# A convolution, router and mixture of experts on one core: later preparation of one visit, another pace of the routing behind the convolution, additions that no longer wait their turn

## The chip, the core and the metric

The kernel runs on one core of a Trainium2 chip. The metric is the device time of one execution in microseconds (us). Engines are named as in the profile: PE (matrix multiply), PEld (its weight loads), DVE (vector), ACT (scalar), POOL (general), SP (issues most DMAs). Each engine takes its instructions strictly in the order in which they were written; a wait holds all that stands behind it on the same engine.

## The reference

`x` is 8 x 2880 x 192. A softmax over 7 taps gives each token and head its own weights, and a causal convolution sums 7 shifted rows with them. Each of the 23040 rows then goes to one of 16 experts (first the best of 4 groups, then the best of 4 experts in it), through two matrices with a ReLU between them, and is scaled by its gate.

```
out = np.einsum('bshk,bskhg->bshg', w, x_unf)          # w: softmax of weight_gen over k (7 taps)
g_idx = np.argmax(x @ w_group, axis=1)                 # group, then expert in the group
e_idx = np.argmax(xg @ w_expert[g], axis=1)
h = np.maximum(xg[mask_e] @ w1[g, e], 0.0)             # 192 -> 1024
ye = h @ w2[g, e]                                      # 1024 -> 192
out[tok_idx] = combined[:, None] * ye                  # gate of the group times gate of the expert
```

## The kernel before

**Front.** Sixteen groups of tokens (12 or 6 columns of 128) go through the convolution on DVE (`conv`: products at L318, additions at L338), the softmax (`softmax`), and the router (`route`), which counts the rows of each expert and gives every row its place. `scatters` writes the rows to a buffer in HBM sorted by expert: for every two columns DVE makes the places (`pair`, L591) and POOL issues two indirect DMAs (L622). Behind the last group `ending` writes 16 pads (L610) after the rows of the 16 experts. `front()` is a generator: each step emits a little DVE work. Three queues hang on it: `side` (softmax), `routes` (router and tables) and `spread` (scatters and pads).

**Visits.** The experts' work is a list of 103 visits in 14 rounds; a round may begin once the rows of certain groups lie in HBM. Visits 0 to 9 take one unit of 128 rows ("plain"), visits 10 to 95 two units (256 rows) of which 86 to 95 are in the last round, and 96 to 102 one unit again. Visits of the last round read rows that all scatters and pads must have reached. A visit is four units of PE work (`u` 0 to 3): in each, `gemm1` (L1021, five terms of high and low parts in a two-unit visit) and, two units later, `gemm2` (L1048, or L1050 and L1051 where the second matrix is split too, visits 52, 57, 61, 64, 68, 70, 72 and 74 to 95). ACT does the ReLU, `finish` scales the sum on ACT (L1057) and, in a split visit, adds the second half on DVE (L1063); then `send` lets POOL scatter the result (L1065). The next `gemm2` needs the accumulator that these free.

**Preparation.** In units 0 and 1 of a visit the next is prepared: `prep_d` copies a part of its rows `xb` to `xd` (ACT L981), `prep_x` transposes them on PE (L997, L998, tile `tpx`), ACT and DVE make `xh` and `xlo`. Weights of a two-unit visit land in `raw` (SP, L910 and L913) and are split on ACT (`hi`, L935 and L938) and DVE (`lo`, L953). The rows `xb` are loaded at L892. SP issues all of these; a load of rows waits on SP until the scatters it depends on have landed.

**Who sets the order.** PE, ACT, DVE and SP run in the order in which Python emits the instructions, and a planner decides that order with a clock of its own, `clk`. `fill(until)` steps `front()` until the planned DVE time reaches `until`; a yielded `NEXT` ends it for this unit. `after`, `delay` and `delay_more` put work on lists that `flush` empties, and each item first calls `fill(t + HOP)`, so front work is emitted ahead of it up to its planned time `t`. `move(queue, q, most)` takes up to `most` steps from a queue entry and stops at one that waits for the next unit. A load is asked for (`ask`) and emitted by `pump` once the planner believes that its rows have come; at unit 0 of a visit `pump(units[...][0])` insists on the next one, and `need` then steps `front()` until its table and rows are emitted:

```
def need(n):
    while not ready(n):
        state["starve"] = True
        more = step() is not False
```

Weights of a visit are asked for by expert number, which the same readiness guards (`if not ready(a[0]) ...: continue`). The last loop of `front()` runs once the convolution is finished; the same happens behind every group through `finish_all`.

Of the kernel before, what the change touches and what calls it, by code (L numbers as in the profile page):

```python
# [34 lines left out]
def conv_moe_kernel(ctx: ExitStack, tc: tile.TileContext, x, wgen, w_group, w_expert, w1, w2, out):  # L35
# [21 lines left out]
    NU = NFT // 2  # L57
# [18 lines left out]
    left = (NTOK - sure + NE * (BK - 1)) // BK  # L76
# [162 lines left out]
    NEXT = object()  # L239
# [60 lines left out]
    def softmax0():  # L300
        wt = grp[0].wt
        m, z = (cv.tile([P, SG * H, 1], F32, name=name, bufs=1) for name in "mz")
        a, b = slice(0, SC * H), slice(SC * H, SG * H)
        for c in (a, b):
            yield from powers(wt[:, c], m[:, c])
        yield from norms(wt[:, a], z[:, a])
        soft0.append([norms(wt[:, b], z[:, b]), None])

    sums, evac, spread = [], [], []
# [433 lines left out]
    def lower_part():  # L743
        t = next(lows[0][0], None)
        if t is None:
            lows.clear()
        else:
            lows[0][1] = t
# [16 lines left out]
    def front():  # L765
        side, routes = [], []
        load_group(0)
        set_up()
        load_group(1)
        yield from softmax0()  # L770
        lows.append([remainders(), 0.0])
        lower_part()
        for g in range(ENDS[-1]):
            o = grp[g]
            routes.append([route(g, o), None])
            state["urgent"] = g == FIRST
            loads = [] if g in (0, ENDS[-1] - 1) else [(0, 0), (8, 1)] if g < MAIN else [(6, 0), (13, 1)]
            ahead = 4 if g <= FIRST else 12 if g < MAIN else 17

            def soft():  # L780
                if not o.ahead and g + 1 < ENDS[-1]:
                    o.ahead = True
                    side.append([softmax(g + 1), None])

            for n, c in enumerate(conv(g, o)):
                yield c
                if loads and n >= loads[0][0]:
                    load_group(g + 1, loads.pop(0)[1])
                if n >= ahead:
                    soft()  # L790
                for q in list(soft0):
                    yield from move(soft0, q, 1)
                if not state["urgent"]:
                    for q in side[:1]:
                        yield from move(side, q, 3)
                for q in spread[:1]:
                    yield from move(spread, q, 1)
                if routes:
                    yield from move(routes, routes[0], HURRY if FIRST <= g < MAIN else 3 if g < FIRST else 8 if g in ENDS else 2)
            while loads:  # L800
                load_group(g + 1, loads.pop(0)[1])
            soft()
            yield from finish_all(side)
            yield from finish_all(routes, 1)
            yield from finish_all(spread, 1)
        while routes:
            for q in spread[:1]:
                yield from move(spread, q, 1)
            q = routes[0]
            yield from move(routes, q, 4)  # L810
            if routes and q[1] is not None:
                yield Until(q[1][1]) if q[1][0] == "time" else NEXT

    def finish_all(qs, keep=0):
        while len(qs) > keep:
# [5 lines left out]
    def move(qs, q, most):  # L821
        for _ in range(most):
            if q[1] is not None:
                what, v = q[1]
                if what == "time" and v > clk["dve"] or what == "unit" and v == state["unit"] and most != HURRY or what == "chunk" and v.o.chunks < v.n:
                    return
                q[1] = None
            c = next(q[0], None)
            if c is None:
                qs.remove(q)  # L830
                return
            if c is NEXT:
                q[1] = "unit", state["unit"]
            elif isinstance(c, Chunk):
                q[1] = "chunk", c
            elif isinstance(c, Until):
                q[1] = "time", c
            else:
                yield c

    fr = front()

    def step():
# [25 lines left out]
    def ready(n):  # L869
        return order[n][:2] in arrive  # L870

    def plain(n):
        return order[n][1] == 1
# [85 lines left out]
    def after(t, cost, note, f, *a, **k):  # L959
        late.append(doing(t, cost, note, f, a, k))  # L960
# [7 lines left out]
    def flush():  # L968
        for q in (late, held):
            while q:  # L970
                q.pop(0)()
        held.extend(later)
        later[:] = far
        far.clear()
# [78 lines left out]
    def finish(b):  # L1053
        for t in range(b.nt):
            gate = b.x[:, t, D:D + 1]
            y = b.x[:, t, 0:D]
            nc.scalar.activation(out=y, in_=b.py[t][:, 0:D], func=AF.Copy, scale=gate)  # L1057
            ty = run("act", 0.3, b.ty)
            after(ty, 0.0 if b.o.whole else 0.35, None, send, b, t, y)

    def send(b, t, y):
        if not b.o.whole:
# [19 lines left out]
    def blocks_of(n):  # L1082
        return max(1, order[n][1] // 2)
# [6 lines left out]
    def blocks(n0, n1, paced):  # L1090
        want, jobs = [], []

        def pump(upto=None):
            for a in list(want):
                if a[1] == 0 and upto is None and ready(a[0]):
                    r = order[a[0]][0]
                    if arrive[order[a[0]][:2]] - (8.0 if r == 1 else 0.0) > max(clk["pe"], clk["dve"]):
                        continue
                if upto is not None and a[0] <= upto:
                    need(a[0])  # L1100
                if not ready(a[0]) or a not in want:
                    continue
                want.remove(a)
                load(*a)
# [34 lines left out]
        units = []  # L1139
# [4 lines left out]
        def block(i):  # L1144
            n, j, _ = units[i]
            o = visits[n]
            b = Slot()
            b.th = {}
            b.plain = plain(n)
            b.nt = 1 if b.plain else 2  # L1150
            b.n = b.nt * P
            b.o, b.h, b.x = o, {}, o.xb[:, 2 * j:2 * j + b.nt, :]
            if not b.plain:
                while state["open"]:
                    assert step() is not False
                state["slots"] = True
            return b
# [29 lines left out]
        for i in range(len(units) + LAG):  # L1187
            if i < len(units):
                n, j, u = units[i]
                gemm1(cur, u)  # L1190
                queue.append((cur, u))
                if i + NU - u < len(units):
                    if u == 0:
                        pump(units[i + NU][0])
                        nxt = block(i + NU)
                        prep_d(nxt)
                    if u == 1:
                        prep_x(nxt, (i + NU) // NU)
                if u == NU - 1 and i + 1 < len(units):
                    cur = nxt  # L1200
            asks = []
            if i >= LAG:
                b, u = queue.pop(0)
                gemm2(b, u)
                if u == NU - 1:
                    finish(b)
                    if i - LAG + 1 < len(units) and units[i - LAG + 1][0] != units[i - LAG][0]:
                        asks.append(units[i - LAG][0] + 3)
            if i < len(units):
                n, j, u = units[i]  # L1210
                nb = blocks_of(n)
                at = j * NU + u
                end = at == nb * NU - 1
                if end and n + 3 < n1 and plain(n + 3):
                    ask_w(n + 3)
                if end and n + 4 < n1 and plain(n + 2) and not plain(n + 4):
                    ask_w(n + 4)
                did = 0
                for job in list(jobs):
                    m, part, h = job  # L1220
                    if m > n + 2 or (part == 3 and (m > n + 1 or at < LAG)):
                        continue
                    must = end and m == n + 1
                    if not must and (did >= 1 or (m, part + (h if part == 3 else 0)) in want or not ready(m)):
                        continue
                    jobs.remove(job)
                    work_split(job)
                    did += 1
                state["unit"] += 1
            flush()  # L1230
            if paced:
                fill(clk["pe"] + AHEAD[0 if cur.plain else 1 if cur.o.whole else 2])
            for a in asks:
                ask_x(a)
            pump()
# [40 lines left out]
```

## Time and profile before

| | |
|---|---|
| median of 3 runs | 1193.42 us (1193.22 to 1197.89) |
| profiled execution, own time | 1198.05 us |
| its span, first to last instruction | 1196.2 us |
| granted clock of PE, mean over the span | 0.986 |
| PE busy, share of the span | 96% |
| DVE, ACT, POOL busy | 80%, 56%, 38% |

The own time is 1.85 us longer than the span. The profiled execution is 4.6 us above the median and close to the slowest of the three timed runs. Times of rows count from the start of the span. A busy PE is not a PE at full clock: where the granted clock is 0.50, the same matmuls take twice as long.

### The profile page before, as it was taken

How to read it: one execution, taken by the hardware profiler on the slowest of the kernel's cores; microseconds unless marked ns; L12 is line 12 of the kernel's file. 1: busy time of each engine (PE TensorE's matmuls, PEld its weight loads, DVE VectorE, ACT ScalarE, POOL GpSimd, SP SyncE). 2: the span in 40 equal slices, each digit the busy share in tenths (PEclk: the TensorE clock that was granted, in tenths of full speed). 3: DMA queues.
4: the chain of work that ended last, by engine and by line, in shares of the span. 5: the costliest groups of instructions: out<-in, count | busy, mean ns of one | idle time of the engine just before them, and what ended most of it. 6: DMA issues, size and time to landing. Idle time of an engine off the chain costs nothing.

```text
span 1196.2 us, 26069 instructions
## 1 busy us (share of the span) xinstructions
PE 1144.0 (96%) x9047; PEld 1113.8 (93%) x9047; DVE 953.2 (80%) x1728; ACT 671.9 (56%) x1267; POOL 455.9 (38%) x411
## 2 busy tenths in 40 slices
PE   4998997999999999999999999999999899999995
PEld 4777997999999999999999999999999899999995
DVE  7987786899999989989899898889876766777600
ACT  2533334655655655656565665655667576777631
POOL 3061350263636253344545253454534443221111
PEclk9999998999999999999999999999999999999998
DMA  9677599989897898888779694899676699887891
GB/s 248 222 234 222 160 311 259 293 245 291 243 284 220 264 272 274 225 276 242 261 215 317 191 301 138 253 281 254 186 212 181 194 283 288 243 221 215 222 257 33
DMA packets 181263, 284.99 MB, mean 238 GB/s; under 512 B 16519, under 2 KB 141293, under 8 KB 180992
## 3 DMA queue, kind: packets, MB, share of 16 engines
q1 hardware_dynamic: 160536, 239.53, 69.9%
q0 software_dynamic: 19184, 39.22, 10.1%
q10 hardware_dynamic: 1400, 4.47, 1.3%
q8 instruction: 73, 1.20, 0.4%
q14 instruction: 70, 0.57, 0.2%
HBM read 239.81 MB, written 44.23 MB: 237 GB/s over the span
## 4 chain that ended last, share of the span: by engine, by line
PE 81%; issue 6%; DMA 5%; DVE 3%; ACT 2%; POOL 1%; ACTq 0%; POOLq 0%; SPq 0%
PE ph L1021 34%; PE py L1048 26%; PE py L1050 6%; PE py L1051 3%; PE pl L409 2%; PE tpx L998 1%; PE tpx L997 1%; DMA raw<-in_moe_w 1%; DMA rows<-xrow,posi 1%; PE tp L437 1%; PE ph L731 1%; DVE pr L318 1%; DMA xb<-rows 1%; PE ph L359 1%; DMA xin<-in_x 1%
## 5 line engine op out<-in xcount | busy, mean ns | idle before, releaser
L1021 PE MATMUL ph<-xh,wa 128*128 128x256 f32 x2064 | 456.0, 298 | 0.0
L1065 POOL DMA_INDIRECT out<-xb x189 | 229.2, 1213 | 521.1 <-ACT xb L1057 321.7
L1048 PE MATMUL py<-wc,hh 128*128 128x192 f32 x2096 | 391.1, 327 | 9.4 <-ACT xb L1057 7.0
L1021 PE MATMUL ph<-xlo,wa 128*128 128x256 f32 x1376 | 356.4, 282 | 1.0 <-DVE xlo L953 1.0
L1021 PEld LDWEIGHTS ph<-xh,wa 128*128 128x128 f32 x2064 | 348.3, 190 | 4.9 <-issue 3.4
L1048 PEld LDWEIGHTS py<-wc,hh 128*128 128x128 f32 x2096 | 336.1, 191 | 9.8 <-ACT xb L1057 7.2
L1027 ACT ACTIVATE hh<-ph 128x512 f32<-128x512 f32 (+1 forms) x296 | 162.3, 548 | 272.0 <-PE ph L1021 270.4
L1021 PEld LDWEIGHTS ph<-xlo,wa 128*128 128x128 f32 x1376 | 259.8, 189 | 1.3 <-DVE xlo L953 1.2
L318 DVE TENSOR_TENSOR pr<-xin,wt 128x1152 f32<-128x1152 f32 x187 | 250.5, 1351 | 8.7 <-PE tpx L359 5.1
L622 POOL DMA_INDIRECT rows<-xrow,pair x138 | 161.7, 1171 | 102.7 <-DVE pair L591 49.3
L338 DVE TENSOR_TENSOR xrow<-xrow,pr 128x1152 f32<-128x1152 f32 x138 | 186.6, 1352 | 0.4
L1050 PE MATMUL py<-wc,hh 128*128 128x384 f32 x464 | 142.8, 363 | 3.4 <-DVE xb L1063 3.4
L953 DVE SCALAR_TENSOR_TENSOR hl<-ph,hh 128x512 fp32r<-128x512 f32 x116 | 80.0, 690 | 74.8 <-ACT hh L1032 74.3
L953 DVE TENSOR_TENSOR wa<-raw,wa 128x1024 fp32r<-128x1024 f32 x86 | 104.7, 1217 | 20.2 <-ACT wa L935 19.4
L1051 PE MATMUL py<-wc,hl 128*128 128x192 f32 x464 | 116.7, 252 | 0.0
L1032 ACT ACTIVATE hh<-ph 128x512 fp32r<-128x512 f32 x116 | 69.5, 599 | 64.4 <-PE ph L1021 64.4
L935 ACT CAST wa<-raw 128x1024 fp32r<-128x1024 f32 x86 | 90.3, 1050 | 12.9 <-DMA raw<-in_moe_w 12.9
L1050 PEld LDWEIGHTS py<-wc,hh 128*128 128x128 f32 x464 | 88.1, 190 | 3.7 <-DVE xb L1063 3.6
L938 ACT CAST wa<-raw 128x1024 fp32r<-128x1024 f32 x86 | 89.7, 1043 | 0.2 <-DMA raw<-w1lo 0.2
L1051 PEld LDWEIGHTS py<-wc,hl 128*128 128x128 f32 x464 | 89.3, 192 | 0.0
L1057 ACT ACTIVATE xb<-py,xb 128x192 f32<-128x192 f32 x189 | 71.0, 421 | 25.1 <-PE py L1048 19.8
L622 POOL DMA_INDIRECT rows<-xrow,posi x42 | 46.0, 1094 | 87.7 <-ACT hl L365 45.1
(181 smaller groups left out, 1342.2 us busy)
## 6 DMA issues: line engine op xcount, KB each, us to landing
wc<-in_moe_w SPq DMA_DIRECT2D x74, 768.0 KB, 7.6
raw<-in_moe_w SPq DMA_DIRECT2D x86, 512.0 KB, 4.9
raw<-in_moe_w SPq DMA_DIRECT2D x96, 256.0 KB, 7.1
xin<-in_x SPq DMA_DIRECT2D x26, 864.0 KB, 9.4
raw<-in_moe_w SPq DMA_DIRECT2D x58, 384.0 KB, 5.2
raw<-w1lo SPq DMA_DIRECT2D x86, 256.0 KB, 6.2
xb<-rows SPq DMA_DIRECT2D x86, 194.0 KB, 4.2
wa<-in_moe_w SPq DMA_DIRECT2D x34, 384.0 KB, 5.7
```

Of the source, the lines that this page charges most:

```text
L318: nc.vector.tensor_tensor(out=dst, in0=o.xin[:, c0 + k:c0 + k + SC, :].rearrange("p s (h g) -> p s h g", g=HG), in1=w4[:, c0:c0 + SC, :, k ...
L338: nc.vector.tensor_tensor(out=acc, in0=acc, in1=prs[k - 2], op=ALU.add)
L622: written_once(nc.gpsimd.indirect_dma_start(out=rows[:, :], out_offset=bass.IndirectOffsetOnAxis(ap=idx, axis=0), in_=src, in_offset=None, ...
L935: nc.scalar.copy(out=o.wa[:, 0, :], in_=o.raw[0])
L938: nc.scalar.copy(out=o.wa[:, 2, :], in_=o.raw[1])
L953: f(*a, **k)
L1021: nc.tensor.matmul(ph[:, v, :], lhsT=w[:, f0:f0 + P], rhs=rhs, start=i == 0, stop=i == len(terms) - 1)
L1027: nc.scalar.activation(out=hh, in_=ph, func=AF.Relu)
L1048: nc.tensor.matmul(b.py[t][:, 0:D], lhsT=hh[:, v, c], rhs=wc[0][:, f, :], start=f == 0, stop=f == NFT - 1)
L1050: nc.tensor.matmul(b.py[t], lhsT=hh[:, v, c], rhs=wc[f // 4][:, f % 4].rearrange("p l d -> p (l d)"), start=f == 0, stop=False)
L1051: nc.tensor.matmul(b.py[t][:, 0:D], lhsT=hl[:, v, c], rhs=wc[f // 4][:, f % 4, 0, :], start=False, stop=f == NFT - 1)
L1065: ins = nc.gpsimd.indirect_dma_start(out=out[:, :], out_offset=bass.IndirectOffsetOnAxis(ap=b.x.bitcast(I32)[:, t, D + 1:D + 2], axis=0), ...
```

## The change

Three edits that do not depend on each other. (1) At the end of `front()`, the loop also runs while `spread` has entries; each pass takes one step of `spread`, routing steps of 1 us in sum, and ends in `NEXT`. Before, it took four steps of routing at a time and did not end a unit by itself. (2) `finish` gives the addition of a split visit the planned time 0.0, so that nothing is filled in ahead of it. (3) In the last plain visit before a two-unit one (visit 9), preparation starts in unit 2 (`turn`), splits of weights wait until then, and two more flushes stand at its end.

```diff
-        while routes:
+        while routes or spread:
             for q in spread[:1]:
                 yield from move(spread, q, 1)
-            q = routes[0]
-            yield from move(routes, q, 4)
-            if routes and q[1] is not None:
-                yield Until(q[1][1]) if q[1][0] == "time" else NEXT
+            left = 1.0
+            while routes and left > 0.0:
+                c = None
+                for c in move(routes, routes[0], 1):
+                    left -= c
+                    yield c
+                if c is None:
+                    break
+            yield NEXT
...
-            after(ty, 0.0 if b.o.whole else 0.35, None, send, b, t, y)
+            after(ty if b.o.whole else 0.0, 0.0 if b.o.whole else 0.35, None, send, b, t, y)
...
-                if i + NU - u < len(units):
-                    if u == 0:
-                        pump(units[i + NU][0])
-                        nxt = block(i + NU)
+                ahead = i + NU - u
+                turn = 2 if ahead < len(units) and plain(n) and not plain(units[ahead][0]) else 0
+                if ahead < len(units):
+                    if u == turn:
+                        pump(units[ahead][0])
+                        nxt = block(ahead)
                         prep_d(nxt)
-                    if u == 1:
-                        prep_x(nxt, (i + NU) // NU)
+                    if u == turn + 1:
+                        prep_x(nxt, ahead // NU)
...
-                    if not must and (did >= 1 or (m, part + (h if part == 3 else 0)) in want or not ready(m)):
+                    if not must and (u < turn or did >= 1 or (m, part + (h if part == 3 else 0)) in want or not ready(m)):
...
             flush()
+            if i < len(units) and turn and u == NU - 1:
+                flush()
+                flush()
```

What this does to the order is seen at three places. The first is DVE around the addition of visit 57 (its rows are `xb_136`, `L1063` before and `L1068` in the change); `m`, `sme`, `smg` and `wt` belong to a softmax and the router, `xrow` and `pr` to the convolution. Before:

```order
L318 TENSOR_TENSOR pr<-xin,wt 128x1152
L272 TENSOR_REDUCE m<-wt 128x96
L274 TENSOR_TENSOR wt<-wt,m 128x672
L532 TENSOR_REDUCE sme<-exe 128x12
L534 SCALAR_TENSOR_TENSOR smg<-sme,smg 128x12
L338 TENSOR_TENSOR xrow<-xrow,pr 128x6x192
L1063 SCALAR_TENSOR_TENSOR xb_136<-py_10243,xb_136 128x192
L1063 SCALAR_TENSOR_TENSOR xb_136<-py_10244,xb_136 128x192
```

Now:

```order
L338 TENSOR_TENSOR xrow<-xrow,pr 128x6x192
L318 TENSOR_TENSOR pr<-xin,wt 128x1152
L1068 SCALAR_TENSOR_TENSOR xb_136<-py_10331,xb_136 128x192
L1068 SCALAR_TENSOR_TENSOR xb_136<-py_10332,xb_136 128x192
L272 TENSOR_REDUCE m<-wt 128x96
L274 TENSOR_TENSOR wt<-wt,m 128x672
```

The two additions have moved ahead of the softmax steps that stood in front of them; the routing steps L532 and L534 are further ahead now, one visit unit earlier.

The second place is POOL at the last pads (L608 reads a place, L610 writes the pad). The rows `out<-xb_135` are the results of visit 80, `xb_136` of 81, and so on to `xb_139` of 84. Before:

```order
L608 TENSOR_LOAD pair
L608 ISA x2
L610 ISA
L610 DMA rows<-pad 128x388
L1065 DMA out<-xb_135 23040x192 x2
L1065 DMA out<-xb_136 23040x192 x2
```

Now:

```order
L608 TENSOR_LOAD pair
L608 ISA x2
L610 ISA
L610 DMA rows<-pad 128x388
L1070 DMA out<-xb_139 23040x192 x2
L1070 DMA out<-xb_140 23040x192 x2
```

The last pad stood ahead of the results of visit 80 and stands ahead of those of visit 84 now. Six pads lie between the results of visit 83 and this place.

The third place is SP at the first load of rows of the last round, `xb6_141` (visit 86; `xb7_142` is 87, `xb0_135` is 88). `raw` rows are weights; `tab2_12591` is the table of the round before the last, `tab2_13594` and `tab2_14065` the last one's before and in the change. Before, where the weights above the load are those of visit 84:

```order
L905 TENSOR_LOAD tab2_12591
L905 ISA x2
L910 ISA
L910 DMA raw00_147<-in_moe_w1 128x1024
L913 ISA
L913 DMA raw10_149<-in_moe_w1 64x1024
L913 ISA
L913 DMA raw10_149<-w1lo_90 64x1024
L891 TENSOR_LOAD tab2_13594
L891 ISA x2
L892 ISA
L892 DMA xb6_141<-rows_89 128x388
```

Now, where the first-matrix weights of visit 85 are the last ones above:

```order
L897 DMA xb6_141<-rows_89 128x388
L896 TENSOR_LOAD tab2_14065
L896 ISA x2
L897 ISA
L897 DMA xb7_142<-rows_89 128x388
...
L897 DMA xb0_135<-rows_89 128x388
L910 TENSOR_LOAD tab2_14065
L910 ISA x2
L915 ISA
L915 DMA raw00_147<-in_moe_w1 128x1024
```

The three loads of rows stand together now, directly ahead of the weights of visit 86 itself; they are emitted in unit 0 of visit 85, together with the last two pads. Before, the load for visit 86 was emitted in the last unit of visit 81.

## Rows read from the trace of the kernel before

**Rows 1.** Waits of PE in the whole run: total us, times, longest us.
```profile
PE py L1048 <- ACT xb L1057: 7.0, 1, 7.0
PE py L1050 <- DVE xb L1063: 3.4, 1, 3.4
PE py L1048 <- DVE xb L1063: 2.3, 1, 2.3
PE tpx L998 <- ACT xd L981: 1.8, 1, 1.8
PE ph L1021 <- DVE xlo L953: 1.0, 1, 1.0
```

**Rows 2.** Timeline 739 to 743: start, duration, operation, [idle before, releaser].
```profile
740.34 1.35 DVE L338 TENSOR_TENSOR xrow<-xrow,pr 128x1152 f32<-128x1152 f32 x1
741.60 0.73 DVE L1063 SCALAR_TENSOR_TENSOR xb<-py,xb 128x192 f32<-128x192 f32 x2
742.07 1.27 PE L1048 MATMUL py<-wc,hh 128*128 128x192 f32 x5 [2.34 <-DVE xb L1063]
```

**Rows 3.** Windows: length, busy of PE, PEld, DVE, ACT, POOL; clock; DMA, GB/s.
```profile
742.10:745.60 3.50, 3.50 (x16) 3.47 (x17) 3.50 (x5) 0.21 (x1) 3.00 (x2) 0.60 0.34 41
952.30:957.80 5.50, 5.46 (x23) 5.46 (x23) 2.80 (x5) 1.41 (x3) 4.08 (x4) 0.50 1.06 313
```

**Rows 4.** Waits of the SP queue, 930 to 1030: total us, times, longest.
```profile
SPq L892 <- DMA rows<-pad: 4.4, 1, 4.4
SPq L892 <- DMA rows<-xrow,pair: 4.2, 1, 4.2
```

**Rows 5.** Timelines 937 to 960 of DVE, POOL, SP, ACT and PE.
```profile
937.72 0.15 DVE L591 SCALAR_TENSOR_TENSOR pair<-pos 128x2 int32<-128x2 f32 x1
940.48 0.68 DVE L953 TENSOR_TENSOR xlo<-tpx,xh 128x512 fp32r<-128x512 f32 x1
939.42 0.97 POOL L622 DMA_INDIRECT rows<-xrow,pair  x1 [0.30 <-issue]
941.98 1.55 SPq L892 DMA_DIRECT2D xb<-rows  x2
944.33 0.33 SPq L910 DMA_DIRECT2D raw<-in_moe_w  x1
944.49 0.41 ACT L981 COPY xd<-xb 128x256 f32<-128x256 f32 x1
949.50 1.04 ACT L935 CAST wa<-raw 128x1024 fp32r<-128x1024 f32 x1 [4.60 <-DMA raw<-in_moe_w]
952.34 0.69 PE L1050 MATMUL py<-wc,hh 128*128 128x384 f32 x1 [3.42 <-DVE xb L1063]
```

**Rows 6.** Timelines 989 to 1005 of POOL and SP: pads and the load behind.
```profile
990.26 0.59 POOL L610 DMA_DIRECT2D rows<-pad  x1
997.34 0.54 POOL L610 DMA_DIRECT2D rows<-pad  x1 [0.77 <-issue]
1004.41 0.35 SPq L892 DMA_DIRECT2D xb<-rows  x1
```

**Rows 7.** Line 610, the pads: time from issue to landing.
```profile
DMA to landing us min/median/max: 5.4/6.9/7.3
```

**Rows 8.** Timelines 1025 to 1033 of POOL, ACT and PE: visit 85 begins.
```profile
1026.40 0.97 POOL L1065 DMA_INDIRECT out<-xb  x1 [0.30 <-issue]
1030.59 0.40 ACT L981 COPY xd<-xb 128x256 f32<-128x256 f32 x1
1032.22 0.27 PE L997 MATMUL tpx<-ident,xb 128*128 128x128 f32 x1
```

**Rows 9.** Timelines 195 to 199 of DVE and PE: the first two-unit visit.
```profile
196.16 0.68 DVE L953 TENSOR_TENSOR xlo<-tpx,xh 128x512 fp32r<-128x512 f32 x1
197.35 1.06 PE L1021 MATMUL ph<-xd,wa 96*128 96x128 f32 x8
198.76 0.53 PE L1021 MATMUL ph<-xh,wa 128*128 128x256 f32 x2
```

## The prediction

> **What bounds the kernel now.** I read the shares of the engines first: PE is busy 96% of the span, DVE 80%, so a change of order pays only where PE stands still or runs at the half clock. The waits of PE [rows 1] are the next view: the reader is to see that five short list entries hold nearly all that the later part of the run loses. 7.0 us is one wait early on (near 180 us), before the code of the change differs: the orders of all engines are equal there up to the last plain visit, so it stays. The other four are the subject: 3.4 us on `py L1050`, 2.3 on `py L1048` for the addition on DVE, 1.8 on `tpx`, 1.0 on `xlo`. The windows [rows 3] add what the list hides: behind a wait of 2.3 us the granted clock is 0.60 for 3.5 us, and behind the one of 3.4 us it is 0.50 (1.2 of 2.4 GHz) for 5.5 us. So a stop costs its length and then 0.40 x 3.5 = 1.4 or 0.50 x 5.5 = 2.75 us. Last, the queue of SP in the stretch behind the convolution [rows 4]: a load of rows stood 4.4 us for the pads and another 4.2 us for the scatters. That queue decides the case.
>
> **Additions not held.** At 740 us DVE runs a convolution addition of 1.35 us ahead of the addition of visit 57, which ends the wait of PE [rows 2]. The order now puts that addition first, with the softmax behind it. ACT's half is done by then in the order of before too, so the wait of 2.34 us and the 1.4 us of slow clock should go: 3.7 us (bounds: 2.3, if something else halves the clock, and 3.7). The 1.0 us on `xlo` [rows 1] had routing steps of DVE ahead of it that now lie elsewhere: -1.0 (bounds 0 and -1.0). What the additions cost DVE, idle time behind ACT, is covered where PE is the bound: DVE has 20% to spare. Without that cover each of the 29 split visits could lose up to a DVE wait, but then the convolution would fall behind, and its order is a product or two ahead of before.
>
> **First two-unit visit later.** `xlo` of visit 10 was done at 196.84, 1.9 us ahead of its first use at 198.76 [rows 9]. Preparation moves by two units; a unit takes 198.76 - 197.35 = 1.4 us, so `xlo` ends at some 199.7, and PE waits 0.9 us (bounds 0, if the two weight splits that moved along clear its way, and 2.8, the whole shift). It is too short a wait to slow the clock, as the 1.0 us on `xlo` was.
>
> **Routing behind the convolution.** This edit moves most. Before, four steps of routing went at once; now a unit gets 1 us, so the tables and the last group's places come later, and the scatters and pads with them. Two loads of rows hang on them.
>
> *Visit 78* (prepared in visit 77). The last scatter it needs ran at 939.42, 1.70 us behind its place on DVE (937.72), and the load of rows left at 941.98, 2.56 us later [rows 5]. In the new order the place stands behind the `xlo` that ended at 941.16: scatter at 942.9, load at 945.4. What followed before is one chain: rows at 944.49 (`xd`), weights behind them on SP at 944.33, their split at 949.50, PE at 952.34. All of it shifts by 3.4 us. The long run of table steps that stood ahead of the addition there is gone now, but ACT's wait for the weights ended later than it, so nothing comes back: +3.4 (bounds 0 and +5, one scatter more or less).
>
> *Visit 86* (prepared in visit 85), the first of the last round. Before, its rows were asked for in visit 81, and SP's 4.4 us for the pads hurt little. Now the last pads and this load are emitted in the same unit, unit 0 of visit 85, and `need` insists. POOL ends the results of visit 83 at 1026.40 + 0.97 = 1027.4 [rows 8], and then has six pads in a row: from the first to the last of such six it took 997.34 - 990.26 = 7.1 us [rows 6], so the last starts at 1034.5. The load left 7.1 us behind the last pad (1004.41), which fits the median landing of 6.9 us [rows 7]: 1041.5. `xd` can start 944.49 - 941.98 = 2.5 us later, at 1044.0. ACT wanted it at 1030.59, and PE stood ready for the transposes at 1032.22 [rows 8]. So the chain of visit 77 repeats with 1044.0 - 1030.6 = 13.4 us more of delay, since there `xd` ran the moment ACT was free. Also, three loads of rows instead of two stand ahead of the weights on SP; two took 944.33 - 941.98 = 2.35 us [rows 5], one more is 1.2. The stop in visit 77 cost 3.42 + 2.75 = 6.2 us [rows 1, 3]. Hence 6.2 + 13.4 + 1.2 = 20.8 us (bounds 15.0 and 24: below, rival 1; above, the slowest landing of 7.3, three more microseconds of POOL waiting on DVE between pads).
>
> A page bears on the landing. The Trainium skill, "DMA: Bandwidth & Descriptors", section "Anatomy of one DMA — SWDGE (gpsimd) path", gives a fixed 2.0 us plus the bytes at 436 GB/s; for the 194 KB of a pad that makes an estimate of 2.5 us. The trace disagrees with 5.4 us at the least [rows 7], so I don't use it; by it the sum would be 4.6 us lower.
>
> *The old wait at 1003* (1.8 us on `tpx`) came while 16 pads and the weights shared the DMA queues. The pads move 40 us on, and may do the same there: -0.9, halfway between gone and moved.
>
> **The sum**, against the profiled execution's own time: 1198.05 - 3.7 - 1.0 + 0.9 + 3.4 + 20.8 - 0.9 = 1217.6 us. That execution lies 4.6 us above the median of the runs; the median of the change should then be **1213 us**, about 1.6% above 1193.42.
>
> **Rivals.**
> 1. *Only the rows hold PE at visit 85, not the weights.* If the weights of visit 86 come as fast as PE takes its short work, the stop is from 1032.2 to the transposes at 1044.4, 12.2 us, plus 2.75 of clock: 15.0 instead of 20.8, and 1207 us. For it: the weights do not depend on pads. Against: they are asked for only once the last round is ready, and SP holds them behind the rows.
> 2. *The pads land fast.* With the 2.56 us of the scatter [rows 5] in place of 7.07, all is 4.5 us earlier: 1208.5 us. Against it, 16 pads in 16 took 5.4 us or more. (This is what the skill's page named above would have.)
> 3. *No new stop at visit 85, not slower.* If the last pad starts 13.4 us earlier, at 1021.1, the rows are there when ACT wants them, and the 20.8 us vanish: 1192 us; the visit-78 term gone as well, 1189 us, or a little under 1187.4. It decides at that start of the last pad: every microsecond behind it is lost whole. For it: the pads are independent of PE. Against: POOL keeps its order, and the results of visit 83, ahead of six pads, cannot be had before 1025.
> 4. *A second stop.* The second matrix's halves and the weights of visit 87 also queue behind the load; if PE stops once more as at visit 77, +6.2: 1219 us.
>
> **Chances.** The forecast 0.62 (its own range 1209 to 1218), rival 1 0.12, rival 2 0.05, rival 3 0.08, rival 4 0.13. The 8-in-10 range reaches from rivals 1 and 2, with the smaller landing, to rival 4 with the larger bound: 1201 to 1222; rival 3 and a tail of rival 4 are left out. This kernel can be told from no change by about 0.5%, 6 us: faster is under 1187.4, slower over 1199.4. Rival 3 has nearly all of what is not slower: 0.04 faster, 0.06 same, 0.90 slower.
>
> **What the profile after would show.** The PE wait for the addition of visit 57 gone and no half clock near 740; a PE wait of 10 us or more on `tpx` for `xd` some 30 us ahead of the end of the split visits, with SP's load of rows waiting for `rows<-pad` and a half clock behind it; a somewhat longer stop near 950; a wait under 2 us at the first two-unit visit. The forecast is wrong if POOL has its six pads out much before PE reaches visit 85, or if the first part of the run gains or loses microseconds of its own, for instance in the 7.0 us wait, whose length other runs may not share.

## The result, and the profile after

The changed kernel takes 1212.74 us in the median of 4 runs (1211.1 to 1218.63), before 1195.66 in 4 (1193.22 to 1198.91): 1.0143 times as long, with a 95% interval of 1.0114 to 1.0171. That is slower, and within 0.3 us of the forecast of 1213. The sum behind the forecast is another matter: its largest term was half as large again as what was measured, and others made up for it.

The profiled execution took 1218.63 us (span 1216.9), 20.6 us more than that of before. Waits of PE in the whole run, total us, times, longest us, after:

```profile
PE ph L359 <- DVE pr L318: 14.0, 2, 13.4
PE py L1053 <- ACT xb L1062: 9.0, 1, 9.0
PE py L1055 <- DVE xb L1068: 7.8, 2, 5.1
PE tpx L1002 <- DMA xb<-rows: 7.6, 2, 6.6
...
PE ph L1026 <- DVE xlo L958: 2.7, 4, 1.1
```

The first row belongs to the start and differs from before by 0.4 us at most. Against [rows 1]: the wait for the addition of visit 57 (`py` in the unsplit form, released by DVE) is gone, as forecast. The early wait for ACT's `xb` is 9.0 us instead of 7.0. The one on the split `py` for DVE's addition has grown from 3.4 to 7.8 in two pieces, 5.1 at visit 78 and 2.7 at visit 85. New is a wait of 6.6 us on `tpx` for rows of the last round. The 1.0 us on `xlo` is still there, among 2.7 in four pieces. The other 1.0 us of the 7.6 on `tpx` stands at visit 78, ahead of the 5.1.

Timelines of POOL, SP, ACT and PE about the start of visit 85 (start, duration, operation, [idle before, releaser]), after:

```profile
1024.47 1.30 POOL L1070 DMA_INDIRECT out<-xb  x1 [0.30 <-issue]
1025.77 1.16 POOL L610 DMA_DIRECT2D rows<-pad  x2
1033.91 1.59 POOL L1070 DMA_INDIRECT out<-xb  x1 [0.30 <-issue]
1035.51 1.75 POOL L610 DMA_DIRECT2D rows<-pad  x3
1040.77 0.54 POOL L610 DMA_DIRECT2D rows<-pad  x1 [0.63 <-issue]
1043.25 2.87 SPq L897 DMA_DIRECT2D xb<-rows  x3
1046.90 0.33 SPq L915 DMA_DIRECT2D raw<-in_moe_w  x1
1045.59 0.41 ACT L986 COPY xd<-xb 128x256 f32<-128x256 f32 x1 [8.26 <-DMA xb<-rows]
1050.99 1.04 ACT L940 CAST wa<-raw 128x1024 fp32r<-128x1024 f32 x1 [4.99 <-DMA raw<-in_moe_w]
1045.61 0.47 PE L1002 MATMUL tpx<-ident,xb 128*128 128x128 f32 x1 [6.59 <-DMA xb<-rows]
1053.83 0.44 PE L1055 MATMUL py<-wc,hh 128*128 128x384 f32 x1 [2.69 <-DVE xb L1068]
```

This is the chain that the prediction wrote out: six pads in a row behind the results of visit 83, the load of rows on SP behind the last, `xd` behind the rows, the weights behind three loads, their cast 4.99 us after ACT was ready, and PE standing twice. The link that is far off is one: the load leaves 2.48 us behind the last pad, where the prediction had 7.1.

Windows of after (length, busy of PE, PEld, DVE, ACT, POOL; clock; DMA share, GB/s), behind the two stops of visit 85, behind that of visit 78, at 742, and last the stretch between the last pad and the load:

```profile
1045.60:1050.80 5.20, 5.19 (x21) 4.93 (x22) 0.00 (x0) 0.40 (x1) 0.00 (x0) 0.50 0.75 240
1053.80:1057.70 3.90, 3.87 (x17) 3.85 (x18) 2.72 (x4) 1.33 (x2) 2.00 (x2) 0.57 1.02 257
960.20:964.50 4.30, 4.30 (x18) 4.30 (x19) 3.31 (x8) 1.23 (x2) 1.94 (x2) 0.50 1.02 213
742.00:750.00 8.00, 8.00 (x62) 8.00 (x62) 5.39 (x13) 4.55 (x9) 2.24 (x2) 1.00 0.86 208
1040.70:1043.20 2.50, 0.00 (x0) 0.00 (x0) 0.00 (x0) 0.00 (x0) 0.54 (x1) 1.00 0.44 159
```

The half clock follows each stop (0.50, 0.57, 0.50), and near 742, where it was 0.60 before [rows 3], it is now full. The stop of visit 85 is thus 6.59 + 2.69 of standing and 0.50 x 5.2 + 0.43 x 3.9 = 4.3 of slow clock: 13.6 us.

**Where the time came from.** Each trace holds the start of 412 ReLU instructions on ACT, one for each unit of PE work. The difference of the same start in two traces, and how it grows from stretch to stretch, says where time is lost; a wait that is caught up again drops out.

| units | what lies there | forecast | measured, after less before |
|---|---|---|---|
| to 34 | start, the early wait; order as before | 0 | +5.4 |
| 34 to 46 | first two-unit visit | +0.9 | +0.5 |
| 46 to 234 | the `xlo` wait at 678 among it | -1.0 | +0.5 |
| 234 to 237 | addition of visit 57 | -3.7 | -4.5 |
| 237 to 308 | | 0 | +2.3 |
| 308 to 320 | visit 78 | +3.4 | +3.9 |
| 320 to 340 | the wait at 1003 | -0.9 | -1.3 |
| 340 to 412 | visit 85 | +20.8 | +13.9 |
| sum | | +19.5 | +20.7 |

### The profile page after: what moved, and what is told of

The parts are those of the page before. It is cut to its first block, busy times and chain, and to the rows that moved or that the text cites. A ratio compares the mean times of both kernels' runs of the same rounds, so it can differ in the third digit from the quotient of the medians.

```text
span 1216.9 us, 26068 instructions
## 1 busy us (share of the span) xinstructions
PE 1149.2 (94%) x9047; PEld 1116.4 (92%) x9047; DVE 952.9 (78%) x1728; ACT 672.4 (55%) x1267; POOL 448.2 (37%) x411
## 4 chain that ended last, share of the span: by engine, by line
PE 69%; issue 12%; DVE 4%; DMA 3%; POOL 2%; ACT 1%; SPq 0%; POOLq 0%; ACTq 0%
PE ph L1026 30%; PE py L1053 25%; PE py L1055 4%; POOL out L1070 2%; DMA raw<-in_moe_w 2%; PE py L1056 2%; PE pl L409 2%; PE tpx L1003 1%; PE tpx L1002 1%; PE tp L437 1%; DMA xb<-rows 1%; DVE xrow L338 1%; PE tp L438 1%; DVE wa L958 1%; DMA rows<-xrow,posi 1%
## 5 line engine op out<-in xcount | busy, mean ns | idle before, releaser
L1070 POOL DMA_INDIRECT out<-xb x189 | 217.9, 1153 | 558.6 <-ACT xb L1062 336.0
L622 POOL DMA_INDIRECT rows<-xrow,pair x138 | 165.1, 1196 | 94.8 <-DVE pair L591 44.7
```

The costliest lines, as they stand in the source:

```text
L622: written_once(nc.gpsimd.indirect_dma_start(out=rows[:, :], out_offset=bass.IndirectOffsetOnAxis(ap=idx, axis=0), in_=src, in_offset=None, ...
L1070: ins = nc.gpsimd.indirect_dma_start(out=out[:, :], out_offset=bass.IndirectOffsetOnAxis(ap=b.x.bitcast(I32)[:, t, D + 1:D + 2], axis=0), ...
```

## The experiments

The runs were made in three groups, each on a chip of its own, and each kernel was timed against the kernel before on that chip. On the first, before took 1196.2 us in the median; on the two others 1250.6 and 1251.3, which no run explains (last section). Ratios hold within a chip; the stretches from unit 234 on are compared with the first trace of before, and on the two slower chips they contain some waits that the profile puts down to nothing in the program ("issue").

**First chip: the edits one at a time.** `e1_loop` is before with the new loop (edit 1), `e2_add` before with

```diff
-            after(ty, 0.0 if b.o.whole else 0.35, None, send, b, t, y)
+            after(ty if b.o.whole else 0.0, 0.0 if b.o.whole else 0.35, None, send, b, t, y)
```

`e3_turn` before with `turn` and its flushes (edit 3), `e4_noloop` the change with the `while routes:` loop of before.

*e1_loop.* 

> The kernel before with the new loop behind the convolution alone. In its order the last pad stands ahead of the results of visit 82 and the rows of visit 86 are asked for six units ahead of visit 85; with the additions of the change as well they stand ahead of those of visit 84 and in unit 0 of visit 85. Theory: the 14 us of the change at visit 85 come from the loop and the additions together, so the loop alone has the rows in time: a PE stop under 3 us at visit 85, some 3 us more at visit 78, 1196 to 1201 us. Rival: the new pace by itself is the loss: a stop of 6 us or more at visit 85 and 1208 to 1215 us.

*e2_add.* 

> The kernel before with the additions of split visits not held, alone. Theory: the PE wait of 2.3 us at 742 and the half clock behind it are gone, all else as before: 4.5 us less than before, 1190 to 1192 us. Rival: the DVE work that is no longer filled in ahead of additions is late elsewhere and takes it back: within 2 us of before, with a new PE wait between 860 and 960.

*e3_turn.* 

> The kernel before with the first two-unit visit prepared later, alone. Theory: 0.5 to 1 us more than before, at 198 to 205 us, as in the change (0.47 us of PE wait for xlo): 1196 to 1197 us. Rival: nothing of it stays, since the wait comes back in the next units: 1195.5 us. The wait of 7 to 9 us near 180 lies ahead of the edit and should vary by as much in this run as in the two known ones.

*e4_noloop.* 

> The changed kernel with the loop of before: the two other edits. Theory: no stop at visit 85, the 742 wait gone: 1191 to 1193 us, under before by 3 to 4 us. Rival: the additions alone delay the pads enough for a stop at visit 85: over 1200 us.

| | ratio to before, 95% | to 34 | 34-46 | 234-237 | 237-308 | 308-320 (visit 78) | 320-340 | 340-380 (visit 85) |
|---|---|---|---|---|---|---|---|---|
| the change | 1.0143 (1.0114 to 1.0171) | +5.4 | +0.5 | -4.5 | +2.3 | +3.9 | -1.3 | +13.9 |
| e1_loop | 1.0065 (1.0037 to 1.0094) | -5.7 | -0.3 | 0.0 | 0.0 | +2.6 | +4.0 | -2.1 |
| e2_add | 1.0040 (1.0015 to 1.0065) | -0.9 | -1.0 | -4.2 | +1.2 | +4.2 | +3.8 | 0.0 |
| e3_turn | 0.9980 (0.9959 to 1.0001) | -4.2 | +0.2 | -4.5 | 0.0 | -0.1 | +1.6 | 0.0 |
| e4_noloop | 1.0043 (1.0026 to 1.0061) | -0.1 | +0.4 | -4.5 | +2.4 | +3.4 | +3.5 | 0.0 |

(The ratio of the change was measured ahead of these; the stretches are those of one trace each.) Four things follow.

The stop at visit 85 needs the loop and the additions together. With the loop alone the last pad stands ahead of the results of visit 82 and the stretch of visit 85 gains instead of losing. Whether it needs edit 3 as well was not run: every kernel that has the stop contains all three edits. Timelines of POOL and SP in `e1_loop`, the last pad, the results of visit 82 and the load:

```profile
1012.16 0.54 POOL L610 DMA_DIRECT2D rows<-pad  x1 [0.64 <-issue]
1013.01 1.02 POOL L1070 DMA_INDIRECT out<-xb  x1 [0.32 <-issue]
1015.79 3.13 SPq L897 DMA_DIRECT2D xb<-rows  x3
```

So my theory for `e1_loop` held in its mechanism. Its median of 1204 us lies above the range that I gave, 8.0 us over before. The trace shows 4.2 us of it from unit 34 on, with 4 us in the stretch from 320 to 340 that I had not counted. It is the trace of the fastest of eight executions (1196.41 to 1209.95), so where the slower ones lose the rest is not shown.

The additions alone do not gain. Their 4.2 us at 742 come as forecast, and then the stop at visit 78 is 4.2 us longer and the waits up to unit 340 another 3.8. In `e4_noloop` it is the same. Both took 1202 us where I had 1190 to 1193, and the rival for `e2_add` (what is no longer filled in comes late elsewhere) had the right mechanism and too small a price. The timeline of POOL, DVE and SP in `e2_add` shows how it goes at visit 78:

```profile
935.03 0.14 DVE L591 SCALAR_TENSOR_TENSOR pair<-pos 128x2 int32<-128x2 f32 x1
934.80 1.10 POOL L1065 DMA_INDIRECT out<-xb  x1 [4.94 <-DVE xb L1063]
936.21 0.97 POOL L1065 DMA_INDIRECT out<-xb  x1 [0.30 <-issue]
937.49 0.97 POOL L622 DMA_INDIRECT rows<-xrow,pair  x1 [0.31 <-DVE pos L556]
938.76 1.74 POOL L622 DMA_INDIRECT rows<-xrow,pair  x1 [0.30 <-issue]
942.13 1.53 SPq L892 DMA_DIRECT2D xb<-rows  x2
```

On POOL in before, the first of the two results at this point:

```profile
940.70 0.97 POOL L1065 DMA_INDIRECT out<-xb  x1 [0.30 <-DVE hl L953]
```

There the scatters (939.42 in [rows 5]) stood ahead of the results. Unheld, the addition goes ahead of the place on DVE, and the two results, at 934.80 and 936.21, ahead of the scatters on POOL. PE is 4.1 us earlier here than in the trace of before at this unit, the place only 2.7 (937.72 in [rows 5]). So the load leaves at 942.13, 0.15 us later than before. What PE won at 742 it waits for at visit 78.

The longer stop at visit 78 comes with the loop alone (+2.6 us) and with the additions alone (+4.2), and the two together give no more (+3.9 in the change). Timelines of DVE, POOL and SP in `e1_loop`:

```profile
934.30 0.68 DVE L958 TENSOR_TENSOR xlo<-tpx,xh 128x512 fp32r<-128x512 f32 x1
934.90 0.15 DVE L591 SCALAR_TENSOR_TENSOR pair<-pos 128x2 int32<-128x2 f32 x1
936.64 0.97 POOL L622 DMA_INDIRECT rows<-xrow,pair  x1 [0.30 <-issue]
939.20 1.54 SPq L897 DMA_DIRECT2D xb<-rows  x2
```

PE is 6.0 us earlier here than in the trace of before. With these added, the place stands at 940.9 directly behind an `xlo`, the scatter at 942.6 and the load at 945.2: the chain that the prediction wrote for this edit (942.9 and 945.4).

The wait at 742 goes with edit 3 too. Timeline of DVE in `e3_turn`:

```profile
733.87 0.34 DVE L538 COPY d<-pl 128x176 f32<-128x176 f32 x1
734.12 0.17 DVE L539 COPY d<-cnt 128x16 f32<-128x16 f32 x1
734.84 0.74 DVE L1063 SCALAR_TENSOR_TENSOR xb<-py,xb 128x192 f32<-128x192 f32 x2 [0.55 <-ACT xb L1057]
```

Two routing steps (L538, L539) stand there where [rows 2] had a convolution addition of 1.35 us. Nothing in that edit is about visit 57: it changes the planned times ahead of it, and the long instruction has moved away. My forecast for this run, up to 1 us more than before, had not seen that. The early wait of 7 and 9 us was 4.0 here and 4.0, 5.2 and 6.9 in the three others, with an order that is the same in all: it alone makes executions differ by 5 us. Behind it, in the two first traces, stands a cast on ACT that waits for its weights to land, 7.90 us before and 11.78 in the change.

**Second chip: size of the pads' part.** `e5_left4` and `e6_pads4` are the change with

```diff
-            left = 1.0
+            left = 4.0
```

```diff
-            if e % 2:
+            if e % 4 == 3:
                 yield NEXT
```

`e7_weights_first` is the change with the weights of the last round's first visit asked for ahead of its rows:

```diff
-            for a in list(want):
+            ahead = upto is not None and order[upto][0] == NR - 1
+            for a in sorted(want, key=lambda a: ahead and a[1] == 0):
```

and `e10_c` is before with four pads in a unit as above and

```diff
-                if not 4 <= g < 8 or s % 2:
+                if not (4 <= g < 8 or g >= 14) or s % 2:
...
+            o.early = n < 74
...
-            after(ty, 0.0 if b.o.whole else 0.35, None, send, b, t, y)
+            after(ty if b.o.whole or not b.o.early else 0.0, 0.0 if b.o.whole else 0.35, None, send, b, t, y)
```

*e5_left4.* 

> The changed kernel with 4 us of routing in a unit behind the convolution in place of 1. Its order has the last pad ahead of the results of visit 82 and the rows of visit 86 in unit 330, eleven units ahead of visit 85. Theory: the stop at visit 85 is the pace of the routing alone, so it vanishes and the kernel is that of the change with the loop of before: 1200 to 1204 us. Rival: a loop that ends every unit costs by itself: 1208 us or more.

*e6_pads4.* 

> The changed kernel with four pads in a unit in place of two: the same places and scatters, the last pad six units earlier in the order, but all 16 still in a row on POOL. Theory, by what the trace of the change shows (a pad 1.1 us on POOL, the load of rows 2.5 us behind the last): last pad at 1035, rows at 1040, 5.7 us earlier, and the stop with its slow clock 6 to 8 us shorter: 1204 to 1207 us. Rival: POOL has no time for them and pads land 7 us late when they come close together, as before the change: 1209 to 1213 us.

*e7_weights_first.* 

> The changed kernel with the weights of visit 86 ahead of its rows on SP, where both are asked for in unit 0 of visit 85. Theory: the first stop of 6.6 us for the rows stays, and ACT's 5.0 us wait for the weights, the second PE stop of 2.7 us and part of the slow clock go: 4 to 5 us less than the change, 1207 to 1209 us. Rival: only the rows hold PE: 1212 us as the change.

*e10_c.* 

> The kernel before with three small edits: additions not held in the split visits up to 72 only, two scatters of groups 14 and 15 in a unit in place of one, four pads in a unit in place of two. In its order the rows of visit 78 are asked for more than seven units ahead of visit 77 in place of at it, and those of visit 86 where before had them. Theory: the waits at 742 (4.2 us with the clock) and at visit 78 (3.4 and 2.75 us) both go and nothing comes for them: 1184 to 1188 us. Rival: what is saved at visit 78 is waited for at visit 86, since the last group's scatters come later: 1191 us or more.

The times expected there were meant for the first chip and cannot be read against these, but their ratios can. Ratios: `e5_left4` 1.0100 (1.0066 to 1.0134), `e6_pads4` 1.0158 (1.0117 to 1.0200), `e7_weights_first` 1.0188 (1.0143 to 1.0233), `e10_c` 1.0045 (1.0019 to 1.0071). Growth from unit 340 to 380: 0.0, +8.7, +14.9 and 0.0 us, against +13.9 and +15.4 in the two traces of the change. So the pace of the routing does decide the stop at visit 85: with 4 us of it in a unit the stop is gone. But `e5_left4` was expected at the ratio of `e4_noloop`, 1.0043, and stands at 1.0100: visit 78 loses 8.2 us there, where the change loses 3.9, and why was not followed up. Pads put closer together shorten the stop by 5 to 7 us, near the 6 to 8 expected, although the load leaves 4.8 us behind the last pad (DMA share 0.69) and not the 2.5 of the theory. `e10_c`, expected 0.7 to 1% under before, is above it.

The weights ahead of the rows changed nothing in sum, and this is the most telling run. Timelines of POOL, SP, ACT and PE, `e7_weights_first`:

```profile
1100.13 0.54 POOL L610 DMA_DIRECT2D rows<-pad  x1 [0.64 <-DMA rows<-pad]
1092.75 0.35 SPq L915 DMA_DIRECT2D raw<-in_moe_w  x1
1106.51 2.80 SPq L897 DMA_DIRECT2D xb<-rows  x3
1108.85 0.41 ACT L986 COPY xd<-xb 128x256 f32<-128x256 f32 x1 [13.52 <-DMA xb<-rows]
1109.16 1.04 ACT L940 CAST wa<-raw 128x1024 fp32r<-128x1024 f32 x1
1108.87 0.48 PE L1002 MATMUL tpx<-ident,xb 128*128 128x128 f32 x1 [11.85 <-DMA xb<-rows]
```

The cast of the weights follows `xd` at once and the second stop is gone, as expected. But PE stands 11.85 us for the rows, since the load leaves 6.38 us behind the last pad. A window of that stretch and one of the same stretch in `e11_change` below:

```profile
1100.10:1106.40 6.30, 0.00 (x0) 0.00 (x0) 0.00 (x0) 0.00 (x0) 0.54 (x1) 0.59 0.72 265
```

```profile
1095.90:1098.30 2.40, 0.00 (x0) 0.00 (x0) 0.00 (x0) 0.00 (x0) 0.54 (x1) 0.82 0.42 152
```

With the weights on their way (DMA share 0.72) the load leaves 6.4 us behind the last pad, without them (0.42, and 0.44 in the first trace of the change) 2.4 to 2.5.

**Third chip.** `e11_change` is the change again. `e8_early_adds` is before with the `o.early` lines above, `e13_early_change` the change with them, `e10_again` is `e10_c`.

*e11_change.* 

> The changed kernel once more, beside the three below. Theory: what lies ahead of unit 34 (visit 9), where the order is that of before, differs by some microseconds, and from unit 42 on the steps are those of the first profile: 4 us less at 742, 3 to 5 more at visit 78, 12 to 16 more at visit 85; in all 1.2 to 1.7% over before. Rival: the stop at visit 85 was that execution's own: under 8 us here, and the change under 1.2% over before.

*e8_early_adds.* 

> The kernel before with additions not held in the split visits up to 72 only; from visit 74 on they are held as before. Theory: it is the additions from visit 74 on that pulled the places, scatters and pads forward, and the early ones cost nothing: 4 us less at 742 and the later waits as before, 0.2 to 0.4% under before. Rival: the gain at 742 is waited for again at visit 78, since the places there hang on DVE and not on PE: within 0.1% of before, with a stop at visit 78 that is 4 us longer.

*e13_early_change.* 

> The changed kernel with the additions from visit 74 on held as before: new loop, later first two-unit visit, additions not held up to visit 72. Its order has the last pad eight units earlier than the change, as with the loop alone. Theory: the 14 us stop at visit 85 needs the new loop and the late additions together, so under 3 us of stop are left there, and the kernel stands 0.2 to 0.6% above before. Rival: the stop stays above 8 us, 1% or more above before.

*e10_again.* 

> The version with early additions, two scatters and four pads in a unit, once more: its first run was in a call in which all kernels, before too, took 55 us longer, with waits for instructions on PE. Theory: without those, the waits at 742 and at visit 78 are gone and it stands 0.5 to 1% under before. Rival: the stretch at units 290 to 296, in which it lost 8 us there, loses them here too: at or above before.

| | ratio to before, 95% | 234-237 | 237-308 | 308-320 | 320-340 | 340-380 |
|---|---|---|---|---|---|---|
| e11_change | 1.0195 (1.0165 to 1.0225) | -4.5 | +3.5 | +4.0 | -0.7 | +15.4 |
| e13_early_change | 1.0153 (1.0117 to 1.0188) | -4.5 | +3.7 | +9.1 | +5.5 | -2.1 |
| e8_early_adds | 0.9989 (0.9966 to 1.0011) | -4.2 | +8.0 | -1.4 | +0.5 | +0.2 |
| e10_again | 1.0013 (0.9989 to 1.0037) | -4.2 | +10.1 | -5.6 | +7.2 | 0.0 |

The change repeats stretch by stretch, at 1.95% over before where 1.2 to 1.7% was expected. In `e13_early_change` the stop at visit 85 is gone, as the theory had it, but not the time: visit 78 and the stretch behind it lose 14.6 us, where the change itself lost 3.3. The theory priced the stop and had nothing for visit 78; what delays it there was not followed up. `e8_early_adds` is not told from before; its 4.2 us at 742 are there and no stop comes at visit 78 (-1.4), but 8.0 us are lost between, and these cannot be separated from this chip's own waits, with no trace of before from it. So neither its theory nor its rival is decided. The same holds for the 10 us that `e10_again` and `e10_c` lose between 237 and 308. They do lose 5.6 us less at visit 78, where their rows are asked for earlier, and lose 5 to 7 us between 320 and 340; `e10_again`, expected 0.5 to 1% under before, is level with it. No version was shown to beat before; the nearest, `e3_turn` at 0.9980, reaches 1.0001.

## Why the prediction was right, and where it was not

**Bound and early part.** That PE's stops decide was right. That the part up to the last plain visit "stays" was right for the order and wrong for a single execution: +5.4 us there belong to no edit, as the four traces of the first chip (-5.7 to -0.1) show.

**Additions.** -3.7 at 742, measured -4.5: right in size. DVE itself stood for ACT ahead of the addition there, and PE did not wait for it, as forecast. Timeline of DVE, after:

```profile
744.73 0.74 DVE L1068 SCALAR_TENSOR_TENSOR xb<-py,xb 128x192 f32<-128x192 f32 x2 [2.54 <-ACT xb L1062]
```

Since edit 3 alone takes the same 4.5 away, the change does not show which of the two did it. The 1.0 us on `xlo` stayed (1.03 before, 0.99 after). The step that failed is "DVE has 20% to spare": the price was not on DVE. An addition that was held had pulled `front()` forward; unheld, it goes ahead of the place, scatters come later against PE, and `e2_add` loses 1.2 + 4.2 + 3.8 us for the 4.2 it gains.

**First two-unit visit.** +0.9, measured +0.5, with a PE wait of 0.47 us on `xlo`.

**Visit 78.** +3.4, measured +3.9. Timelines of DVE, POOL and SP there, after:

```profile
944.61 0.68 DVE L958 TENSOR_TENSOR xlo<-tpx,xh 128x512 fp32r<-128x512 f32 x1
945.20 0.15 DVE L591 SCALAR_TENSOR_TENSOR pair<-pos 128x2 int32<-128x2 f32 x1
946.91 0.97 POOL L622 DMA_INDIRECT rows<-xrow,pair  x1 [0.30 <-issue]
949.47 1.54 SPq L897 DMA_DIRECT2D xb<-rows  x2
```

The place stands behind an `xlo`, and with 4.1 us less, PE's shift at this unit, the second scatter is at 942.8 and the load at 945.4, against 942.9 and 945.4 in the prediction. The size and the chain were right, and `e1_loop` shows both under the loop alone, as the heading "routing behind the convolution" has it. What the prediction lacked is that the additions alone give a stop of this size too, so the change does not show which of the two makes it.

**Visit 85.** With PE's shift of 6.6 us ahead of it taken off, the last pad started at 1040.77 - 6.6 = 1034.2 (forecast 1034.5; luck in part, since the results ahead ended 1.5 us later than forecast and the six pads took 5.3 us and not 7.1), ACT was ready for `xd` at 1045.59 - 8.26 - 6.6 = 1030.7 (forecast 1030.6), and the weights followed the load of rows by 3.65 us (forecast 2.35 + 1.2). The mis-sized term is the landing: 7.1 us taken from [rows 6, 7], measured 2.48. This is what rival 2 said, and its price of 4.5 us is most of the 6.9 by which 20.8 exceeds 13.9. Another 1.1 us is the landing of the weights: their cast starts 4.09 us behind their issue, and 5.17 in [rows 5]; the rest is not assigned. The rows of before were not wrong, they were read where other transfers shared the DMA engines. Window of before from the last pad to the load:

```profile
997.30:1004.40 7.10, 5.27 (x42) 5.04 (x41) 3.12 (x5) 4.44 (x8) 2.54 (x3) 1.00 0.96 277
```

The DMA share is 0.96 there and 0.44 in the same stretch of the change, where SP itself stands in front of the weights and the last pad has the DMA engines more nearly to itself. The pads' own crowd is not it: the last six of the change follow each other faster (5.3 us) than those of before (7.1). All twelve traces in which SP's load waits for the pads agree. With the share taken exactly from the last pad's start to the load's (0.39 then in the two traces of the change), the load leaves 2.4 to 3.7 us behind it at shares of 0.39 to 0.44, 3.6 to 4.8 at 0.62 to 0.69, 6.4 to 6.9 at 0.71 to 0.78, and 7.1 to 7.3 at 0.88 to 1.03. The Trainium skill, "DMA: Bandwidth & Descriptors", section "Anatomy of one DMA — SWDGE (gpsimd) path", from which the prediction made an estimate of 2.5 us and put it aside, agrees with the two traces of the change and not with those where the DMA share is 0.62 or more.

**The forecast's luck.** 1213 against 1212.74 is nearer than the sum deserves: visit 85 was 6.9 too large, and 2.3 (units 237 to 308), 1.5 (46 to 234) and the early 5.4 were not in it.

## What to carry to other kernels

Look at what a wait pulls along before calling its removal free: here holding an instruction was what kept another stream ahead, and undoing it cost more at the next dependency than it saved. When a price is taken from a row, ask whether the same transfers will share the queue in the new place; a pad cost 7 us among weights and 2.5 nearly alone. And two edits that each cost half a per cent can meet in one deadline, so sum them on the new order, not apart.

## What the runs showed of the hardware

The same kernel before took 1196 us on one chip and 1251 on two others. Waits of PE that were put down to issue, `e11_change` on the third chip:

```profile
PE tp L437 <- issue: 7.9, 5, 2.8
PE py L1053 <- issue: 6.4, 2, 6.2
PE ph L1026 <- issue: 4.1, 3, 3.2
PE ph L359 <- issue: 3.1, 3, 1.1
```

Nothing that the profile shows ended them. All of them come to some 30 us, and to 22 to 30 in every kernel of these two chips, while no trace of the first chip has one on PE. DVE shows them too (10 to 29 us, none on the first chip), and ACT 27 to 38 (5 to 8 on the first). They come mostly ahead of unit 200: by then `e11_change` stands 60.7 us behind the first chip's trace of before (the first trace of the change 7.9), 30 of them in such waits of PE, and from unit 234 on it loses as the change did there. What these waits are (the text on `e10_again` calls them waits for instructions), and where the rest goes, is not shown.
